# Output groups of a local attention inside the loop of a dense one: from one block of 15 full-row matmuls to five pieces of row halves

## The chip, the cores and the metric

The kernel runs on one core of a Trainium2 chip. The core has five engines that run side by side, each on its own queue of instructions: TensorE (PE, matmuls, with its weight loads as PEld), VectorE (DVE), ScalarE (ACT), GpSimd (POOL) and SyncE (SP), which here issues the DMA transfers. An engine works its queue off in order; it waits at an instruction until the semaphores say that its inputs are there and its output buffer is free. Matmuls write to PSUM, which has eight banks of 128 partitions x 512 columns of fp32; ACT and DVE read PSUM, POOL does not.

The metric is the device time of one execution in microseconds (us); lower is better. The time given is the median of several runs.

## What is computed

Two attention blocks over 2048 positions of 640 features, with 32 heads of 20, whose outputs stand side by side. Attention A looks at eight earlier positions, two apart; attention B at all positions.

```python
def _A_ref(x, wqkv, wo):                      # W, dil = 8, 2
    q, k, v = split_heads(x @ wqkv)           # 32 heads of 20
    idx = pos[:, None] - arange(8) * 2        # masked where negative
    attn = softmax(where(mask, einsum("bhsd,bhswd->bhsw", q, kg) * scale, -1e9))
    o = einsum("bhsw,bhswd->bhsd", attn, vg)
    return merge_heads(o) @ wo

def _B_ref(x, wqkv, wo):
    q, k, v = split_heads(x @ wqkv)
    p = softmax(einsum("bhqd,bhkd->bhqk", q, k) * scale)
    return merge_heads(einsum("bhqk,bhkd->bhqd", p, v)) @ wo

return concatenate([a, b], axis=-1)
```

## The kernel before

All matmuls of the projections are made exact enough by splitting each operand into a rounded high part and the rest, and summing three products (`PASSES`: high x high, high x low, low x high). A projection of 640 features is five contraction chunks (`KC`) of 128, so one output group of 128 rows x 320 columns is 15 matmuls into one PSUM bank: `rows15`.

**Stages.** First come A's projections of q, k and v (stored to DRAM), then B's q and k, then B's values (`v_group`). In the last of these the 15 matmuls are already made as row halves where `halves` is set: the contraction rows 0 to 63 and 64 to 127 are two matmuls on two halves of the array, into two banks; ACT copies both out of PSUM and POOL adds them. Then comes the long loop, then a tail that finishes B and writes its output.

**The loop.** It runs B's attention in units of four heads by 512 queries by 128 keys: 512 steps in all, of which the loop makes 488. Each step needs four half-row matmuls of scores (PE, 62 contraction rows, 512 columns) with an exponential each on ACT, and one set of value matmuls (`b_pv`, eight in the trace). Every second step ends a sum of values, which ACT copies out and POOL adds to the running sum (braw). The scores need the maximum of each query, and that is computed 24 steps ahead (`LEAD`) with score matmuls of its own (60 rows, 512 columns), which DVE reduces over the columns: four halves to a step as well, and three small DMAs bring the maxima back as extra rows of q.

**The order is written out by hand** in the string `ORDER`, from line 955 on, which is read token by token. A token names what PE does next and the PSUM banks that it uses:

- S: two halves of scores, each with its exponential. M: two halves of maxima in neighbouring banks, with one reduction of 1024 columns. N: the same in any two banks, with two reductions of 512. Y: one half of scores and one of maxima, with one exponential and one reduction of 512. Each is a pair of matmuls on the two row halves of the array, at the same time.
- V: the next step. `begin(i)` (which calls `tick`, so that work laid down with `after(n, ...)` becomes due) and then the value matmuls, into the bank that the token gives, if any.
- F: one output group of A, into the bank that it names. j: one of the five transposes of a tile of A.

**Attention A in the loop.** A's local attention is elementwise work on POOL (`a_attention`), in units that `begin` deals out: it emits the next unit as long as POOL's planned time (`gp.us`, a sum over the instructions emitted so far) is less than the step's time plus `AHEAD`. DVE makes its softmax's maximum and reciprocal, ACT its exponential. A finished tile of 128 rows is transposed by DVE (`j`), goes through DRAM, is split by POOL into `aot` (one buffer, `turn_parts`), and is then in `ready_a`. Each tile gives two output groups (two halves of 320 columns), 32 in all. `a_out` makes one: a bank, `rows15`, and `store_rows` with ACT's copy into a tile "ro" (tag "r", three buffers) and, one step later, the store to DRAM. A group named by F before its tile is ready is kept in `owed` and made at the next V.

When all groups of A are made (`left_a`), B's output weights are loaded into the same buffers as A's (`load_out(wo_b, ...)`); they are used after the loop.

The profile puts nearly all instructions on line 66, the helper `emit` that records them, so they are told apart by their tiles: `mx<-ps_st` are reductions for maxima, `e<-ps_st` exponentials, `bq,bk` and `bk,bq` score matmuls for maxima or exponentials, `e,vb` values, `ww,aot` A's output groups, `ww,xn` and `ww,xl` B's values, `ro` the copied outputs, `braw` and `more` the sums of values, `akv`, `al` and `am` attention A's operands, scores and maxima.

Of the kernel before, what the change touches and what calls it, by code (L numbers as in the profile page):

```python
# [10 lines left out]
F32 = mybir.dt.float32  # L11
# [7 lines left out]
H = 32  # L19
# [3 lines left out]
KC = 5  # L23
# [47 lines left out]
def attention_pair(ctx, tc, xa, wqk_a, wv_a, wo_a, xb, wqk_b, wv_b, wo_b, oa, ob):  # L71
# [720 lines left out]
    def b_token(kind, ns):  # L792

        m = None
        if kind == "S":
            what = [s_half(), s_half()]
        elif kind == "Y":
            o = s_half()
            if m_open[0] is None:
                m_open[0] = m_two()  # L800
                what = [o, (*m_open[0], 1 - o[3])]
            else:
                m, m_open[0] = m_open[0], None
                what = [o, (*m, 1 - o[3])]
        else:
            m = m_two()
            what = [(*m, 0), (*m, 1)]
        b_two(what, ns if len(ns) == 2 else (ns[0], ns[0] + 1), kind == "M")
        if m:
            m_done(m)  # L810
# [43 lines left out]
    def v_group(n, half, s, halves=False):  # L854
# [13 lines left out]
        if halves:  # L868
            more = sb.tile([128, 320], F32, tag="r", bufs=3, name="more")
# [42 lines left out]
    outs = iter(())  # L912
    fill = []

    def out_piece():

        nonlocal outs
        if next(outs, 0) is None:
            return True
        outs = a_out(WO)  # L920
        return next(outs, 0) is None
# [6 lines left out]
    def begin(i):  # L928
# [31 lines left out]
        "Y06S52M3Y17V6S05jM3Y21VY70S52M3S16N70V5S41M2Y67VY04S36M1S75N04V3S27Y61N05VY74S06jM1jN35jF7jY06M1S35S74V0M5Y31"  # L960
        "S72VY73S64M1Y50V3Y47M1S65VY07M5S41Y23V0Y17M5S42VY71M3S25S06N17V2Y03S14M5VY70M3S15S26N07V1Y25S04N36VY07S25N43"
        "Y61V0Y72N54S36VY71M5S23N40F7Y61M2S45Y07V6Y51M2S04VY70M4S13Y26V7Y03M4S21VS06M2S14N57V0Y16N23S45VS74M5M1N03F7Y62"
        "S01M4Y73V6Y02M4S71VY70M2S14Y56V7Y04M2S15VY06M4S13Y72Y60V1Y75M3S26VY07S62S53jN41N70jF6jjjY70M1S35Y46V7Y05M1S34V"
        "Y03M5S41S72N30V4Y57S36M1VY07M5S31Y42V7Y03S61Y54VM2S04Y16V5S07M2Y46VY70M2S14S65N70V1S26M3Y75VY06S72M3Y51V0Y72"
        "S63M4VY71M2S64Y05V7Y64M2S01VY06M4S13Y72Y60V1S75M3Y26VY07S25M3S61Y07V2M3Y56S71VN03S74M5S12S07N34V1Y02S35M6VY02"
        "M3Y57N61Y20F5Y74S63M1Y05V7Y64M1S03VS06M4S31N72V0S36M4Y71VM2S76Y45V1Y07S26N34VY07M2S65Y41V7Y06M2S54VY06M4jS13j"
        "S27jN60jF1jY72S03M4Y61V7Y02M4S63VY06M1S35S74N60V3Y72S16M4VY70M1S64Y35V0Y74S16M2VY71M4S63Y20V7Y61M4S32VY06M2S14"
        "S75N60V1Y72S36M4VY07M2S64S51N70V6Y52M3S71VS70M1S53N46V7S05M1Y34VS05Y63Y21N74V0S13M5Y72VS13M5S74Y02V1Y73M5S24V"
        "Y07M2S46S51N70V4Y35M6S21VY05M1S37N64N50F3Y74M1S56Y03V7Y64S52M0VY63M4S20S71Y36V2M4S07N16VS05Y74Y31V2Y04M5S71V"
        "Y70S34M5Y12V7S03N64Y51VjS06jM4M2S17F0jjjY71S26M4Y03V7Y62M4S01VY06M2S14Y75V0Y16M2S74VY71M5S42S30N17V4Y35S62M0V"  # L970
        "Y73M5S20Y14V7S03M5Y21VY03S24M5Y17V0Y24M5S13VY74M1S36S05N47V3Y02S41M5VY70M1S46S35N07V4Y36M1S05VY07Y63S52M0S74"
        "N63V5S70M1Y64VS70M1Y36S45V7M1S03Y46VY05S13Y24N67V0S13M4Y62VS71M4Y63N20F7Y61S02M4Y73V6Y02M4S71VY70M2S14S56N07V1"
        "Y25S04N36VY07S25M3S61N07V2S36M4Y01VY73M4S06Y12V7Y06M4S31VY06M2S14Y75V6Y04M2S17VY05S71jM2jS46jN50jF7jY06S51M2"
        "Y74V0Y15M2S76VS71M4S63N02V7S61M4Y03VS62M0S54N73V6S50Y12Y74VM2S01Y45V7Y60M2S15VY06M4S31S27N60V3Y24M5S71VY70M1"
        "S46S35N07V4Y36M1S05VY07M5S31S42N70V3Y41M5S72VY70M1S46S35N07V4Y36M1S05VY07M5S31S42V7M0Y63S45VM0S26S34N57V2Y30"
        "S16N54VY70M5Y13N42F0Y71M5Y43S02V7Y04M5S12VY04M1S35Y76V0Y53M1S74VY73M5S42S01N37V4Y05S36M1VY07M5S31S42N70V3S41j"
        "M5Y72VS04jY71M5M2F0jjY71S26M4Y03V7Y62M4S01VY06M2S14S75N60V1Y72S36M4jVS07M2S64Y51V0M6S23Y41VY73S26M4S10N37V2Y16"
        "M4S30VY73M0S64Y52V7Y63M0S45VY62M3S50Y17V2Y65M3S01VY07M5S14S32N70V1S36M4Y72VY03S74M5S21N03V7S62Y54M0VY62S35N40"
        "N71S62V3S04M5Y72VS04M5Y71N23F0Y71M5Y42S03V7S01M5S43VM0S26Y54V3Y70M1S46VY07S45M1S63N70V4Y51M6S32VM0S25M6S34Y20"
        "Y15V3Y42M6S01VY02S14M6Y53V2Y01M6S45VjS01jM4M6S32jF0jjY71M4S63Y02V7Y61M4S03VY06M1S35S74N60V3Y72M5S41VY70M1S46"  # L980
        "S35N07V4Y36M1S05VY07M5S31S42N70V3S41M5S72VM0S74Y56V2Y73M0S46VY73M4S06S12N37V0Y16M4S32VY71M2S64Y05V7Y64M2S01V"
        "Y06M4S13S27N60V1Y25M3S76VY07M5S24S31N70V2Y36S75Y14VM6Y05S43V1Y02S76M4VN07M2M4S61F0Y71S62M4Y03V7Y62M4S01VY06M2"
        "S14S75N60V1Y72S36M4VY07M2S64S51N70V6Y52M3S71VS70M1S53N46V7S05M1Y34VS05Y63M1Y74V0S35jM1Y76VS53S74jM1N06F5jjjY07"
        "S61M2Y45V0Y17S62M3VY71M5S24S03N17V2Y06S15M3VY07M5S14Y32V7S01M5Y43VY02S16M4S37N02V1Y36M4S07VY06M2S74S15N06V7S41"
        "M2S05VY64S03M1V5Y46S70M1VY74S63M1S05N47V6Y03M1S54VY70M4S31Y26V7Y03M4S21VS06M2M4Y17F0Y16S52M3Y70V1Y26M3S75VY07"
        "M5S24S31N70V2S36M4Y71VY03S74M5Y12V0Y73M5S14VY71M2S46S50N17V4Y35M1S06VY07M5S31S42N70V3Y41M5S72VS70M1S46N53V7S04"
        "M1Y65VjS04jS36M1Y75jF0jjY71M2S46Y05V7Y64M2S01VY06M4S13Y72V0Y13M4S76VY71M2S64Y50V1Y76M2S45VY07M4S63S21N07V6S52"
        "M3Y01VY75M3S02Y16V7Y05M3S21VY02M5S14Y73V2Y01M5S47VY01M3S75S62N10V7Y63S45M1VY06M3S52S71N60V5Y74S63M1VS07M3S62"
        "Y51V0S74Y36M1VY74M5S31S02N47V3Y06S45M1VY07M4Y61N23F0Y71S26M4Y03V7Y62M4S01VY06M2S14S75N60V1Y72S63M4VY07M2S64S51"
        "N70V6Y52S73N41VY70S52M3Y16V7S05jM3Y21VS06jM3Y52N17F0jY16S52M3Y70V1Y26M3S75VS07M5S24Y31jV0jM5S72Y14VY73S26M4Y10"  # L990
        "V3Y27M4S61VY07S61M4S23N70V6Y51S72M3VY70M1S53Y46V7Y05M1S34VY03M5S41S72N30V4Y57S36M1VY07M5S31S42N70V3Y41M5S72V"
        "Y70S14M5S32N07V1Y63M4S02VY07M2S64S51Y70V6M2S54Y01VN75S42M0S36Y74V5Y32M0S67VY64M2M0Y75F6Y74S03M1Y56V7Y04M1S35V"
        "Y06M3S52S71Y60V5Y74M2S01VM6S04Y32V1Y07M5S24VY07S23Y46N51V7S06M2Y54VS06jS51jM2N47F0jjjY71S26M4Y03V7Y62M4S01VY06"
        "M2S14S75N60V1Y72S36M4VY07M2S64S51N70V6Y52M3S71VS70M1S53Y46V7M1S05Y63VY02S14M5V3Y70S21M5VY70S14M5S23N07V1Y26M4"
        "S03VY07M2Y64S51V0Y75S63M1VY74M5S31S02N47V3Y06S45M1VY07M4S61S32N70V6Y51M3S72VS70M1S53Y46V7Y05M1S36VY03S45M1M6"
# [122 lines left out]
```

## Time and profile before

| | |
|---|---|
| runs, median of 3 (lowest to highest) | 1767.14 us (1765.48 to 1768.25) |
| profiled execution | 1766.22 us |
| its span, first to last instruction | 1764.4 us |
| instructions | 32352 |
| granted TensorE clock | 0.999 |

How to read it. The profile shows one execution. A row of the engines gives busy time, its share of the span and the number of instructions. The slices of the page divide the span in 40 equal parts; each digit is the busy share in tenths:

```profile
PE   9999999999999999999999999999999999999999
PEld 8988888898344444444444444444444444444569
DVE  3100232368999999999999999999999999999300
ACT  4222322233999999999999999999989999999981
POOL 0000058335899999999999999999999985355242
```

The projections take the first ten slices, the loop the next 27 or so, the tail the rest. Matmuls are pipelined and their ends are modelled, so a busy PE is not PE at its peak. In a view of groups a row gives the number of instructions, their busy time (overlaps counted once), the mean of one in ns, and the idle time of the engine just before them with what ended it. In a timeline a row gives start, length, engine, operation and how many instructions it merges, with the idle time before it in brackets; the start of the next row minus this row's start is what the work cost the engine's queue, since the ends of pipelined instructions overlap the next ones.

### The profile page before, as it was taken

Reading aid. Unit: us, or ns where it says so; the run is one execution under the profiler, and the core shown is the slowest. Engines: PE = TensorE matmul, PEld = TensorE weight load, DVE = VectorE, ACT = ScalarE, POOL = GpSimd, SP = SyncE. Lnnn points to the kernel's source line nnn. Section 1 sums busy time; section 2 is a strip of 40 time slices with the busy share of each in tenths; the row PEclk is TensorE's granted clock in tenths of the full one; section 3 lists DMA queues with packets and bytes.
Section 4 is the critical chain, followed back from the end, with each engine's and each line's share of the span. In section 5 each row is a group of like instructions: output and inputs, shape, how many; then the busy total and the mean of one; then the engine's idle time right before and its main releaser. Section 6 shows DMA issues by size and latency. Waiting matters only on the chain.

```text
span 1764.4 us, 32352 instructions
## 1 busy us (share of the span) xinstructions
PE 1751.5 (99%) x11571; PEld 996.1 (56%) x11571; DVE 1336.5 (76%) x1813; ACT 1330.0 (75%) x2617; POOL 1228.0 (70%) x1096
## 2 busy tenths in 40 slices
PE   9999999999999999999999999999999999999999
PEld 8988888898344444444444444444444444444569
DVE  3100232368999999999999999999999999999300
ACT  4222322233999999999999999999989999999981
POOL 0000058335899999999999999999999985355242
PEclk9999999999999999999999999999999999999999
DMA  6333596863644454364445345453644432122123
GB/s 231 114 98 110 174 312 245 270 183 116 179 135 136 118 150 124 123 168 124 129 138 153 124 120 160 116 155 102 177 133 128 129 114 72 38 71 58 33 71 115
DMA packets 191194, 240.27 MB, mean 136 GB/s; under 512 B 89020, under 2 KB 115260, under 8 KB 190040
## 3 DMA queue, kind: packets, MB, share of 16 engines
q1 hardware_dynamic: 190456, 237.54, 44.6%
q8 instruction: 91, 1.49, 0.4%
q10 hardware_dynamic: 576, 0.66, 0.1%
q14 instruction: 71, 0.58, 0.1%
HBM read 173.21 MB, written 64.91 MB: 135 GB/s over the span
## 4 chain that ended last, share of the span: by engine, by line
PE 88%; POOL 6%; DMA 2%; DVE 1%; ACT 1%; issue 1%; SPq 0%; POOLq 0%; ACTq 0%; DVEq 0%
PE ps_st L66 88%; POOL akv L66 3%; POOL braw L66 1%; DVE mx L66 1%; ACT e L66 1%; DMA bk<-kb_d 1%; POOL ww L66 1%; SPq L66 0%; DMA stg<-wo_a 0%; DMA vb_d<-ve 0%; POOL aot L66 0%; POOL al L66 0%; DMA s_d<-braw 0%; DMA akv<-ka_d 0%; DMA qb_d<-pr 0%
## 5 line engine op out<-in xcount | busy, mean ns | idle before, releaser
L66 DVE TENSOR_REDUCE mx<-ps_st 128x1 f32<-128x512 f32 (+1 forms) x1491 | 1215.1, 881 | 37.5 <-PE ps_st L66 32.8
L66 ACT ACTIVATE e<-ps_st 128x512 f32<-128x512 f32 x2048 | 1063.6, 619 | 31.2 <-PE ps_st L66 12.9
L66 PE MATMUL ps_st<-bq,bk 62*128 62x512 f32 x2048 | 552.7, 439 | 2.7 <-DVE mx L66 1.2
L66 PE MATMUL ps_st<-e,vb 128*32 128x512 f32 x4096 | 543.0, 604 | 0.6
L66 PE MATMUL ps_st<-bk,bq 60*128 60x512 f32 x2048 | 532.5, 438 | 3.0 <-DVE mx L66 2.0
L66 PEld LDWEIGHTS ps_st<-bq,bk 62*128 62x128 f32 x2048 | 277.4, 184 | 446.3 <-ACT e L66 285.5
L66 POOL TENSOR_TENSOR braw<-braw,more 128x512 f32<-128x512 f32 x224 | 288.0, 1286 | 93.1 <-ACT more L66 92.9
L66 POOL TENSOR_TENSOR akv<-akv,aq 128x1280 f32<-128x1280 f32 x64 | 189.0, 2953 | 233.7 <-DVE w L66 233.7
L66 PEld LDWEIGHTS ps_st<-bk,bq 60*128 60x128 f32 x2048 | 248.8, 184 | 85.6 <-DVE mx L66 47.9
L66 POOL TENSOR_TENSOR akv<-akv 128x640 f32<-128x640 f32 (+3 forms) x304 | 282.4, 929 | 14.3
L66 ACT COPY ro<-ps_st 128x320 f32<-128x320 f32 (+2 forms) x124 | 61.3, 496 | 223.0 <-PE ps_st L66 173.7
L66 PEld LDWEIGHTS ps_st<-e,vb 128*32 128x32 f32 x4096 | 82.1, 108 | 153.0 <-ACT e L66 74.1
L66 POOL TENSOR_TENSOR akv<-akv,al 128x1280 f32<-128x1280 f32 x64 | 152.0, 2375 | 0.2
L66 ACT COPY more<-ps_st 128x512 f32<-128x512 f32 (+1 forms) x248 | 144.5, 583 | 2.3 <-PE ps_st L66 1.5
L66 PE MATMUL ps_st<-wc,xn 128*128 128x512 f32 (+1 forms) x576 | 133.4, 376 | 0.0
L66 PE MATMUL ps_st<-ww,xn 64*128 64x320 f32 (+1 forms) x1056 | 125.8, 311 | 0.4 <-ACT ve L66 0.4
L66 PEld LDWEIGHTS ps_st<-ww,xn 64*128 64x128 f32 (+1 forms) x1056 | 116.8, 187 | 14.1 <-ACT e L66 8.0
L66 PEld LDWEIGHTS ps_st<-wc,xn 128*128 128x128 f32 x576 | 106.3, 188 | 17.6 <-ACT xn L66 0.3
L66 PE MATMUL ps_st<-xn,w 128*128 128x512 f32 x480 | 115.8, 390 | 0.0
L66 PEld LDWEIGHTS ps_st<-xn,w 128*128 128x128 f32 x480 | 90.1, 188 | 19.4
L66 ACT CAST pr<-ps_st 128x512 fp32r<-128x512 f32 x40 | 23.5, 587 | 101.4 <-PE ps_st L66 101.4
L66 DVE TENSOR_TENSOR pr<-ps_st,pr 128x512 fp32r<-128x512 f32 x40 | 27.7, 692 | 92.7 <-ACT pr L66 92.7
(65 smaller groups left out, 1010.3 us busy)
## 6 DMA issues: line engine op xcount, KB each, us to landing
akv<-ka_d SPq DMA_DIRECT2D x128, 320.0 KB
akv<-va_d SPq DMA_DIRECT2D x128, 320.0 KB
kb_d<-pr SPq DMA_DIRECT2D x20, 512.0 KB
qb_d<-pr SPq DMA_DIRECT2D x20, 512.0 KB
bk<-kb_d SPq DMA_DIRECT2D x16, 640.0 KB
bq<-qb_d SPq DMA_DIRECT2D x64, 160.0 KB
rb<-s_d SPq DMA_DIRECT2D x128, 64.0 KB
stg<-xb SPq DMA_DIRECT2D x12, 512.0 KB
```

The costliest lines, as they stand in the source:

```text
L66: return self.tc.keep_in_program_order(op(*a, **k))
```

## The change

An output group of A in the loop is no longer one block. The token F is gone; a token H with two banks stands for one of five pieces of a group. A piece is one contraction chunk: three passes, each as two matmuls of 64 contraction rows on the two row halves of the array, into the two banks. All five pieces of a group name the same two banks and stand between two V, with S, M, N and Y tokens among them. After the fifth piece ACT copies both banks into two tiles, POOL adds them one step later, and the store is issued four steps later (before: one step after the copy). The tag "r" has four buffers instead of three, everywhere that it is used.

The order string is another one from step 37 or so on: where groups and transposes stand and which tokens with which banks surround them. Its counts, before and after: S 661 and 641, Y 630 and 670, M 509 and 530, N 152 and 111, V 488 and 488, j 80 and 80, F 32 and none, H none and 160. `b_token` is cut in two without a change of what it does.

```diff
     def store_rows(p, dst):
-        r = sb.tile([128, 320], F32, tag="r", bufs=3, name="ro")
+        r = sb.tile([128, 320], F32, tag="r", bufs=4, name="ro")
...
-    def a_out(W):
-
-        while ready_a and ready_a[0][0] <= now[0]:
-            _, t, ot = ready_a[0]
-            for half in range(2):
-                if half:
-                    ready_a.clear()
-                p = bank()
-                rows15(p, lambda xi, k: ot[:, xi, k], W[half])
-                store_rows(p, oa[t * 128:(t + 1) * 128, half * 320:half * 320 + 320])
-                left_a[0] -= 1
-                yield
+    unit = []
+
+    def out_chunk(ns):
+
+        if not unit:
+            unit[:] = [0, *ready_a[0][1:], left_a[0] % 2]
+        k, t, ot, half = unit
+        for i, (wi, xi) in enumerate(PASSES):
+            for r, n in enumerate(ns):
+                rows = slice(r * HALF, r * HALF + HALF)
+                pe.matmul(psb[:, n, :320], ot[rows, xi, k], WO[half][wi][rows, k],
+                          start=(k == 0 and i == 0), stop=(k == KC - 1 and i == 2))
+        unit[0] += 1
+        if unit[0] < KC:
+            return
+        unit.clear()
+        left_a[0] -= 1
+        if half:
+            ready_a.clear()
+        o, more = [sb.tile([128, 320], F32, tag="r", bufs=4, name="ro") for _ in range(2)]
+        for to, n in zip((o, more), ns):
+            act.copy(to, psb[:, n, :320])
+        after(1, pool, o, o, more, ALU.add)
+        after(4, sp.dma_start, oa[t * 128:(t + 1) * 128, half * 320:half * 320 + 320], o)
...
-        "Y06S52M3Y17V6S05jM3Y21VY70S52M3S16N70V5S41M2Y67VY04S36M1S75N04V3S27Y61N05VY74S06jM1jN35jF7jY06M1S35S74V0M5Y31"
...
+        "Y06S52M3Y17V6Y05M3S21VY70M1S53S46jY07V5jY41S32M6jVjM0S43H76H76Y52H76Y01Y34H76Y52H76jM0S34V5M6S32Y01VM6S42Y03V1"
+        "S24M6Y50VY24S73M5Y01V2Y73M5S04VM0S73Y46H52H52Y70Y13H52Y46H52Y70H52M3Y16V7S05M1Y34VY06S51M2Y47V0Y16S52M3VY71M5"
...
     def out_owed():
 
-        while owed:
-            given.append(owed[0])
-            if not out_piece():
-                given.clear()
-                break
-            owed.pop(0)
+        while owed and (unit or ready_a and ready_a[0][0] <= now[0]):
+            out_chunk(owed.pop(0))
...
-        elif kind not in "FV":
+        elif kind == "H":
+            owed.append(ns)
+            out_owed()
+        elif kind != "V":
             b_token(kind, ns)
-        elif kind == "F":
-            owed += ns
-            out_owed()
```

More of the change, by code (lines that the diff above doesn't have):

```diff
@@ L790, in m_done, with take @@
             max_end(u * NKB + NKB - 1)
-    def b_token(kind, ns):
+    def take(kind):
         m = None
@@ L807, in b_token @@
             what = [(*m, 0), (*m, 1)]
+        return what, m
+    def b_token(kind, ns):
+        what, m = take(kind)
         b_two(what, ns if len(ns) == 2 else (ns[0], ns[0] + 1), kind == "M")
@@ L868, in v_group @@
         if halves:
-            more = sb.tile([128, 320], F32, tag="r", bufs=3, name="more")
+            more = sb.tile([128, 320], F32, tag="r", bufs=4, name="more")
             act.copy(more, ps2[1][:, :320])
@@ L909, in attention_pair @@
     assert next(steps, None) is None
-    outs = iter(())
     fill = []
[L915 to L921, printed above, removed]
     WO_b = []
@@ new lines, in attention_pair @@
+        "N56S71VY72Y13H45Y06H45S72N13H45S06H45Y72H45M0Y63V2M4S01Y76VS01M4Y73V6Y02M4S17VY03H71N24S65H71Y03H71Y26H71Y54"
+        "H71M2Y06V5Y74S03M1VS07M3N62S51V0S73M4Y16VS73M1Y45V0Y76M1S34VY73M5S42S10N37V4S56M1Y03VY75S06M1Y34V7Y06S51M2Vj"
+        "S06jM4S13Y72jV0jY16S54M2jVY71M5S42S30N17V4Y35S62M0VY73M5S20S14N37V2Y01M5S34VY70M3Y15S62V7Y60S14M2M5S01VS04M2"
+        "S15M6V0S14M2M6S15VY14M2S57Y06V4Y51M2S70VY75M0S62S34N57V6Y03M1S54VY70M4Y31S26Y07V3Y24M5S01VY70Y14S25H36H36Y71"
+        "H36N02S45H36Y71H36Y04N52V7S61M3Y05VY61S02M3Y57V6Y02S13M4VY70M1S35Y46V0Y75M1S34VY73M5S42Y10V3Y47M5S21VY70H42S15"
@@ new lines, in attention_pair @@
+        "N36H42S70H42Y31H42Y57H42M0Y36V7Y52S01M3VY06M1S53Y47V6S50jM1S34jVjY70S51M2V4jY07S56M2jVY70S15M2S64N07V1M2S65Y04"
+        "VM5S72S03Y41M5N72S10V3S41M5Y70VM1S74S56N03V7Y24M0S65VY62S35M0Y47V6Y53M0S24VY75M2S40S16N57V4Y03M1S56VY07M5S31"
+        "S42N70V3Y41M5S72VM0S72S46N53V7M0S24Y65VM2S04H16H16Y75H16Y04Y23H16H16M4S70M2V1S74M5VM2S07H45Y61H45H45Y07Y32H45"
+        "Y61H45Y07N32V6S75M0Y43VY75S04Y12N63V7S02M4Y61VY02S36M4Y17V0Y62M4S13VY71M2S64S05N17V6Y04M2S51VY70M4S13S26N07V1"
+        "Y25M3S06VS07M5S24Y31V0jY72M5S14VjM2S71Y46V5jY70M2S16VY70S61M2S45N07V6Y41M2S05VY70S15Y42Y36S07M1jV5jY64M1S03V"
@@ new lines, in attention_pair @@
+        "VM2S16H50Y47H50Y13Y62H50Y74H50Y13H50M6Y42V1S03M4Y76VM2S07Y45V6Y70M2S14VY70M4S13Y26V0Y71M4S32VY71M2S64H50H50Y17"
+        "H50Y64Y32H50Y17H50M3Y62V1S07M5Y43VY07M5S42Y31V0Y72M5S43VY74M1S36Y05V4S37jM1Y60VS75jM1S63Y04jV7jM1S65Y43VM1S06"
+        "Y54V3Y07M1jS65VY07M5S41S23N07V4S56M1Y03VM5S70M1S34V7Y06M3S52M0S65VY62M3S50S71N26V5Y70M3S21VY07M1S63S45N70V6Y14"
+        "M2S75VY70M4S13S26N07V1Y25M3S06VY07M5S24S31N70V2Y36M4S71VY07Y16M4S32S70V1M2S46Y75VM2S04H67H67Y51H67Y04Y32H67Y51"
+        "H67M3Y02V5S67M0Y43VY72M0Y64S35V7Y63M0S25VY62M3S50Y71V6Y05M3S72VY70H51Y24H51Y06Y73H51Y24H51Y06H51M2Y74V0S15M6"
@@ new lines, in attention_pair @@
+        "Y23VY14S72M5Y30V1Y27M5S43VY07M3S25Y61V7S02jM3Y56VY02S13M4S67Y02jV1jM4S63Y27VjM4S03M6jS21V0Y25S43M6VS15M3M6S20"
+        "V1S25M3M6S02VY05M3S27S61N05V2S37Y64M0VS73M4S60N12V7Y63S45M0VY62M3S50S71N26V5Y70M3S21VY07M1S63S45N70V6Y14M2S75V"
+        "Y70S15Y42Y36N07V1S26M4S03VM6S05Y42V3N07S61N52VM6S01H45H45Y03H45Y21Y67H45Y03H45H21M6H21S03M4H21H21M6S03H21N54V0"
+        "Y73S12M5VS71M3S25N06V7S41M2Y05VS64M0S23N75V6S04M1Y73VS05M1S74N36V0Y71S25M3VY71M5S24Y03V1Y27M5S40VjY72M3S05S61"
+        "Y72jV0jM3S56jY12VY73S64M1S50N37V6S51jM3Y02VY71S05M3S26N71V0S25M3Y76VY51Y72Y34M5S01S72V3Y40S15M6VM0S24S75N63V2"
@@ new lines, in attention_pair @@
+        "Y70S16M4VY70S16M4Y32V0Y17M4S63VY71M2S64Y50Y17V6Y52S34M0VY75M2S40S16N57V4Y03M1S56VY07M5S31Y42V7Y03S61M4VY06S13"
+        "H24N57H24S06H24Y35H24Y70H24M5S31N07V2S36M4Y01VY73S04M5Y12V7Y03M5S41VY04M2S15Y76V0Y15M2S74VS71M5S42N30V7M5S41"
+        "Y23VY04M5H12Y37H12S04H12N35S60H12Y74H12Y36N05V7S64M1Y03VS46M1S05Y73V4jY06M1S35VjM6S03Y21V5jY04M6S31VjY04M2S17"
+        "Y65V4Y70M2S16VY70M5S13S24N07V1Y26S05M3VM6S05M3S21V0Y72M5jS14VY71S24M5S30N71V2Y36M4S70VY73S06M4M1S73V0Y74M5S31"
+        "S27M3VS12M5S74N03V1S27M5Y04VS73M5S02N14V7S06Y53M1VY06M3S57S21Y06V5Y74M2S61VN07S64M2S15S06N74V1Y02S73M5VY07M2"
@@ new lines, in attention_pair @@
+        "M3Y21VY06S52M3Y17V0Y62M3S15VY71H26Y35Y04H26Y71H26Y35H26Y70H26M3Y15V7S60M1Y34VY06S51M2Y47V0Y16S52M3VY71M5S24Y03"
+        "V1Y27S64N50VN72S36H54Y01H54Y73H54Y62Y01H54H54M6Y32V0Y15M6S43VY15M3S27Y06V5Y12S74N30VY76S41M2Y05V6Y74M2S10VY75"
+        "M0S42H36H36Y75H36Y42H36Y70H36M4Y21V7Y06S52M3VY06M1S53Y74V0Y35M1S76VY73M4S62S10N37V6S51M3Y02VY71S05M3S26N71V0"
+        "S25M3Y76VY15M3S72S60N15V7S64M2Y01VY64S05M2S17N64V0S15M2Y76VY15S74M2Y60V1Y75M2S46VY07M4S63Y21V0Y73M4S62VS71M2"
+        "S64N05V7S63M1Y04VS35Y06M1S74N36V5S70M1Y43VY07S64M1S35N07V6S41M2Y05VY74M2S01S56N74V0Y15M2S76VY71M4S63S02N71V6"
@@ L1014, in attention_pair @@
+        "S05M3Y72VY05M3S71S26N05V7Y41M2S06VY01S64Y53S72N01V6M3S50Y71VM3S05M1S76")
     owed = []
     def out_owed():
-        while owed:
-            given.append(owed[0])
-            if not out_piece():
-                given.clear()
-                break
-            owed.pop(0)
+        while owed and (unit or ready_a and ready_a[0][0] <= now[0]):
+            out_chunk(owed.pop(0))
     i = 0
@@ L1078, in attention_pair @@
         out_matmuls(p, qc, n, (KC - 1,))
-        r = sb.tile([128, 320], F32, tag=("r", "p")[n > 1], bufs=(3, PB)[n > 1], name="ro")
+        r = sb.tile([128, 320], F32, tag=("r", "p")[n > 1], bufs=(4, PB)[n > 1], name="ro")
         (act.copy if n % 2 else dve.tensor_copy)(r, p[:, :320])
```

77 lines of the change are left out of this document (24 added, 53 removed).

## The prediction

> **What bounds the kernel now.** I read the page from the top (busy shares, slices, chain), then the stretches, then the groups of the busiest engines, then single moments. The page alone points to PE:
>
> ```profile
> PE 1751.5 (99%) x11571; PEld 996.1 (56%) x11571; DVE 1336.5 (76%) x1813; ACT 1330.0 (75%) x2617; POOL 1228.0 (70%) x1096
> PE 88%; POOL 6%; DMA 2%; DVE 1%; ACT 1%; issue 1%; SPq 0%; POOLq 0%; ACTq 0%; DVEq 0%
> ```
>
> PE is busy for 99% of the span and 88% of the chain. Both count pipelined matmuls whose ends are modelled, so the stretches must decide. The first row below is the loop before the first output group, the second the loop with the groups, the third the loop after them, the fourth the tail without maxima (columns: stretch, length, then each engine's busy time):
>
> ```profile
> 430.00:530.00 100.00, 98.79 (x659) 43.16 (x659) 96.20 (x128) 91.29 (x183) 92.05 (x85) 0.98 0.53 152
> 530.00:1560.00 1030.00, 1025.77 (x7054) 463.81 (x7054) 1010.45 (x1400) 956.92 (x1894) 937.49 (x816) 1.00 0.44 126
> 1560.00:1646.00 86.00, 85.59 (x588) 34.87 (x584) 85.02 (x115) 83.19 (x165) 48.56 (x49) 1.00 0.22 63
> 1646.00:1764.40 118.40, 114.27 (x799) 86.01 (x792) 8.26 (x16) 71.40 (x147) 35.89 (x34) 1.00 0.26 81
> ```
>
> The loop lasts some 1216 us (430 to 1646), 2.49 us for each of its 488 turns. In it DVE is busy 96.20 + 1010.45 + 85.02 = 1191.7 us and idle 24.3; ACT is idle 84.6 and POOL 137.9. Does PE have room? One turn's values, and a scores run, show what its work costs start to start:
>
> ```profile
> 902.30 1.07 PE L66 MATMUL ps_st<-e,vb 128*32 128x512 f32 x8
> 903.29 0.50 PE L66 MATMUL ps_st<-bq,bk 62*128 62x512 f32 x1
> ...
> 396.12 0.65 PE L66 MATMUL ps_st<-bk,bq 60*128 60x512 f32 x4
> 396.61 1.92 PE L66 MATMUL ps_st<-ww,xn 64*128 64x320 f32 x24
> 398.36 0.60 PE L66 MATMUL ps_st<-ww,xl 64*128 64x320 f32 x6
> 398.80 0.67 PE L66 MATMUL ps_st<-bk,bq 60*128 60x512 f32 x4
> ```
>
> Eight value matmuls take 903.29 - 902.30 = 0.99 us, a pair of half-row matmuls (396.61 - 396.12) / 2 = 0.245. A turn needs one such eight and on average four pairs: 0.99 + 0.98 = 1.97 us of 2.49, and 0.16 more for its share of the groups. PE has about 0.36 us a turn to spare. So in the loop DVE sets the time, with 2% of slack, and the other engines only matter where they let it run dry.
>
> A rule of the Trainium skill bears on this choice: Trace Analysis ("Perfetto Trace Analysis", section "Identifying the Most-Contended Engine") says that matmul occupancy is no good measure of nearness to the roofline, because PE's instructions are pipelined. By it PE's 99% is no bound and DVE is; without it PE is the bound and the second rival below is the forecast.
>
> **What the change removes: the long block.** In the loop an output group is 15 full-row matmuls in one piece. One of them, as PE, ACT and DVE saw it:
>
> ```profile
> 880.62 2.47 PE L66 MATMUL ps_st<-ww,aot 128*128 128x320 f32 x15
> 883.02 0.50 PE L66 MATMUL ps_st<-bq,bk 62*128 62x512 f32 x1
> ...
> 883.12 0.43 ACT L66 COPY ro<-ps_st 128x320 f32<-128x320 f32 x1 [1.59 <-PE ps_st L66]
> ...
> 880.27 2.92 DVE L66 TENSOR_REDUCE mx<-ps_st 128x1 f32<-128x512 f32 x3
> 883.11 0.48 DVE L66 STREAM_TRANSPOSE turn<-ao 128x128 f32<-128x128 f32 x2
> ```
>
> The block holds PE 883.02 - 880.62 = 2.40 us. ACT starves for 1.59 of it, but DVE lives through it on maxima laid up before. Where the stock was short, DVE paid:
>
> ```profile
> 1538.75 1.82 DVE L66 TENSOR_REDUCE mx<-ps_st 128x1 f32<-128x512 f32 x2 [1.87 <-PE ps_st L66]
> ...
> 1559.20 3.02 DVE L66 TENSOR_REDUCE mx<-ps_st 128x1 f32<-128x512 f32 x4 [1.22 <-PE ps_st L66]
> ...
> 1406.89 0.60 DVE L66 TENSOR_REDUCE am<-al 128x32 f32<-128x256 f32 x1 [2.22 <-POOL al L66]
> ```
>
> The first two follow the groups at 1535.8 and 1556.2. All of DVE's waits for PE in the stretch with the groups, from the view of the PSUM tile:
>
> ```profile
>   PE ps_st L66: 11.9, 31
> ```
>
> So 11.9 us in 31 waits is the most that a smoother supply can give back there; the third row is a wait for POOL, which nothing in the change removes.
>
> How much smoother is it? I counted both orders between tokens that feed DVE (M, N, Y), with 0.99 for a V, 0.245 for a pair, 2.40 for an old group, and for a new piece a fifth of the half-row run above, (398.80 - 396.61) / 5 = 0.44. Old: 62 silences over 1.6 us, 32 of them (the groups) of 2.65 to 2.89. New: 20 over 1.6, none over 1.73. The group's own PE time falls from 2.40 to 2.19, and the run above goes from half-row scores into half-row pieces and back without a gap, so cutting it in five costs PE nothing. Per turn with a group, old: 32 turns need 32 x (0.99 + 2.40) + 263 pairs x 0.245 = 172.9 us of PE and carry 289 halves of maxima, which last DVE 289 x 2.49 / 4 = 179.9. New: 30 turns (two hold two groups) need 30 x 0.99 + 32 x 2.19 + 259 x 0.245 = 163.2 and carry 287, 178.7. The margin doubles, 7.0 to 15.5. I take half of the 11.9 as given back: **-6.0**. Ends: nothing, and all of the loop's idle from 530 on, (1030 - 1010.45) + (86 - 85.02) = **-20.5**; below nothing stands in the rivals.
>
> **What the order adds or removes by itself.** Both orders hold 1952 halves of scores, 1952 of maxima, 488 V and 80 transposes. The maxima are packed otherwise: 530 reductions of 1024 columns for 509, 892 of 512 for 934.
>
> ```profile
> L66 DVE TENSOR_REDUCE mx<-ps_st 128x2 f32<-128x1024 f32 x509 | 616.5, 1215 | 3.0 <-PE ps_st L66 2.0
> L66 DVE TENSOR_REDUCE mx<-ps_st 128x1 f32<-128x512 f32 x933 | 602.4, 682 | 18.0 <-PE ps_st L66 14.2
> ```
>
> Busy time by count is 1.211 and 0.646: 21 x 1.211 - 42 x 0.646 = 25.4 - 27.1 = **-1.7**, all on DVE, so all on the path. By the means (1215 and 682, which overlap) it is -3.1.
>
> **What is hidden.** Each group gets a second ACT copy and a GpSimd addition:
>
> ```profile
> L66 ACT COPY ro<-ps_st 128x320 f32<-128x320 f32 x32 | 13.7, 427 | 47.6 <-PE ps_st L66 47.6
> ...
> L66 POOL TENSOR_TENSOR ve<-ve,more 128x320 f32<-128x320 f32 x24 | 19.3, 812 | 74.8 <-ACT more L66 73.0 <-DMA vb_d<-ve 1.7
> ...
> SPq L66 <- ACT ro L66: 183.1, 31, 14.4
> ```
>
> ACT: 32 x 0.427 = 13.7 us, on an engine with 84.6 idle in the loop, 47.6 of them before these very copies: nothing on the path. If that cover were gone, 13.7. POOL: 32 x 0.812 = 26.0 us. POOL is 91% busy from 530 to 1560, but a half empty after that (48.56 of 86), and attention A's work is dealt out by POOL's planned time: the additions push it back by 26 us, ten turns, and the last group moves from turn 450 to 458 of 488. Attention B's output weights, loaded after it, are needed only from turn 488. Nothing, while POOL keeps up; behind a late addition stand akv's products, A's softmax (for which DVE waits: the 2.22 above, once) and the braw sums. The upper end: such a wait at each of 15 softmaxes, 15 x 2.22 = 33.
>
> The store moves from one turn after the copy to four turns behind, after the addition. On SP's queue that is past the akv fetches, the q and k loads and the maxima's stores; the queue now stands 183.1 us in 31 waits for the copies because the store is issued early, so moving it back frees the queue rather than blocks it. Its number, 32, stays. Behind it wait akv loads (POOL) and the maxima's way back, needed 24 turns later. The r buffers go from three to four: two groups in one turn need just four. All of this I take at nothing.
>
> **Sum.** 1.7 + 6.0 = 7.7 less. The profiled execution took 1766.22 (span 1764.4 and 1.8 around it), 0.92 below the median of the runs, 1767.14. 1766.22 - 7.7 = 1758.5, and on the runs' median **1759.4**.
>
> **Rivals.**
>
> 1. *No change, 1764 to 1770.* DVE's small waits are spread over all of the loop (31 with a mean of 0.38), and a new order has as many of its own; or pieces come before their group is ready, are owed, and run together at the next V, so that the block stays a block. Then the packing alone is left, -1.7: 1765.4. For it: 20 silences of 1.73 remain, and during a group two of eight banks are gone. Chance 0.22.
>
> 2. *PE is the bound after all.* Then 32 x (2.40 - 2.19) = 6.7 counts, 1760.4; or, with all of the loop's idle won back, 1767.1 - 1.7 - 20.5 = 1744.9. For the first the chain's 88%, against it PE's spare 0.36 us a turn. Below 1750: 0.08.
>
> 3. *Slower: the banks.* A group holds two banks through some ten tokens, and the sums of the values one more; five are left for scores and maxima, where before a block held one bank for 2.40 us. If DVE cannot have a second maximum waiting while PE does an eight and a pair (0.99 + 0.245 + 0.245 = 1.48), it runs dry by what it lacks: a 512 reduction in hand lasts 0.646, so up to 0.83 a group, 32 x 0.83 = 27: 1767.1 - 1.7 + 27 = 1792 at worst. It decides from (1.7 + 3.5) / 32 = 0.16 a group on, and half of the worst, 0.4, gives 1778. Against it: the orders put M or N, two halves, right before most of the longer silences. Chance 0.10.
>
> 4. *Slower: evacuation.* Two banks must be emptied where it was one. If ACT had no room, its 13.7 us would count in full, with no gain beside the packing: 1767.1 - 1.7 + 13.7 = 1779. ACT's 84.6 us of idle time speak against it. A POOL that falls behind (up to 33) ends in the same region. Chance 0.06. On this the Trainium skill speaks against the change: TensorEngine Tiling (Array Packing), section "PSUM Bottleneck", warns that tiling speeds up TensorE but not the emptying of PSUM, so that the copies may become the bottleneck; by it the time would be this rival's, while by the row's idle time the sum stands.
>
> **How the numbers follow.** The forecast case (DVE stays the bound, 3.5 to 17 us gained) has 0.54. 0.2% is 3.5 us, about what a measurement of this kernel can tell from no change. Faster by more: 0.54 + 0.08 = 0.62; within: 0.22; slower: 0.10 + 0.06 = 0.16. The range leaves out 0.08 below 1750 and the slower cases' upper two thirds: 1750 to 1771.
>
> **What would show it.** Right: ACT's wait before the ro copies falls from 47.6 to under 15, DVE's idle time from 530 to 1646 from 20.5 to about 14, its reductions are 530 and 892, the tail after the last maximum still takes 118 us, matmuls of 64 rows from aot come in runs of six with pairs of scores between. Wrong: DVE waits for PE inside the new groups (rival 3), am waits for al more than once (rival 4), or DVE's idle time stays at 20 (rival 1).

## The result: 9 us less, and where they came from

The changed kernel takes **1758.29 us** (median of 5 runs, 1756.04 to 1760.11) against 1767.64 for the kernel before: ratio 0.9947, 95% interval 0.9932 to 0.9961. The profiled execution took 1756.04, 10.2 less than the profiled one before.

The loop up to the last reduction of maxima, and the tail behind it, before (columns: stretch, length, then busy time of PE, PEld, DVE, ACT and POOL):

```profile
430.00:1649.30 1219.30, 1212.76 (x8304) 543.01 (x8304) 1194.95 (x1645) 1134.70 (x2246) 1079.38 (x950) 1.00 0.43 123
1649.30:1764.40 115.10, 111.66 (x781) 84.83 (x781) 4.98 (x11) 68.10 (x141) 34.62 (x33) 1.00 0.27 84
```

The same two stretches after:

```profile
430.00:1639.10 1209.10, 1197.67 (x8783) 547.38 (x8783) 1192.85 (x1624) 1146.20 (x2278) 1104.99 (x982) 1.00 0.43 124
1639.10:1754.30 115.20, 111.68 (x782) 84.86 (x782) 4.98 (x11) 68.10 (x141) 34.65 (x33) 1.00 0.26 83
```

All of the gain lies in the loop; the tail is the same to 0.1 us. DVE's idle time in the loop fell from 24.35 to 16.25 us, 8.1 of the 10.2; the other 2.1 is busy time. From 530 to the last reduction the idle time fell from 20.5 to 13.7. What DVE waited for after, in the view of the PSUM tile over 530 to 1560 (before: 11.9, 31):

```profile
  PE ps_st L66: 5.4, 10
```

Over the whole loop, three waits before (time, number, longest), and the same three after:

```profile
DVE mx L66 <- PE ps_st L66: 16.2, 40, 2.1
DVE am L66 <- POOL al L66: 2.2, 1, 2.2
...
PE ps_st L66 <- DMA bq<-mdr: 0.7, 1, 0.7
```

```profile
DVE mx L66 <- PE ps_st L66: 8.0, 17, 1.4
DVE am L66 <- POOL al L66: 3.6, 1, 3.6
...
PE ps_st L66 <- DMA bq<-mdr: 3.6, 3, 1.8
```

So the waits for PE halved, and two others grew: DVE's one wait for POOL, and PE's for the DMA that brings maxima back.

Where the waits for PE stand in the timelines says more than their sum. Before, from 530 on, 24 of DVE's waits end 2.9 to 3.0 us behind the start of a group, 10.1 us together, and ten others are 2.4. After, four waits of 0.16 to 0.27 stand in a group, at its start or right behind it, 0.8 us together. The five longest after, 4.5 us together, stand behind three stops of PE, at 1215 and 1295 for the maxima's DMA and at 1429, which is followed below. So nearly all of what the block cost DVE is gone, and more than half of what is left is new.

A group after the change, on PE:

```profile
646.82 0.60 PE L66 MATMUL ps_st<-ww,aot 64*128 64x320 f32 x6
647.26 0.42 PE L66 MATMUL ps_st<-bk,bq 60*128 60x512 f32 x2
647.49 0.42 PE L66 MATMUL ps_st<-bq,bk 62*128 62x512 f32 x2
647.73 0.63 PE L66 MATMUL ps_st<-ww,aot 64*128 64x320 f32 x6
```

Six matmuls hold PE for 647.26 - 646.82 = 0.44 us, and pairs of scores follow without a gap. The groups of DVE and ACT that answer to those before:

```profile
L66 DVE TENSOR_REDUCE mx<-ps_st 128x2 f32<-128x1024 f32 x532 | 642.7, 1215 | 3.0 <-PE ps_st L66 1.7
L66 DVE TENSOR_REDUCE mx<-ps_st 128x1 f32<-128x512 f32 x892 | 576.0, 681 | 8.8 <-PE ps_st L66 6.3
...
L66 ACT COPY ro<-ps_st 128x320 f32<-128x320 f32 x64 | 24.6, 449 | 0.1
```

ACT no longer waits before the copies (47.6 us before, 0.1 now), but its waits for PE before the exponentials grew, so that about half of that time moved and did not go. Before and after:

```profile
ACT e L66 <- PE ps_st L66: 12.9, 52, 1.2
```

```profile
ACT e L66 <- PE ps_st L66: 38.6, 79, 3.2
```

### The profile page after: what moved, and what is told of

Same layout as the page of the kernel before. It is cut to its first block, busy times and chain, and to the rows that moved or that the text cites. A ratio compares the mean times of both kernels' runs of the same rounds, so it can differ in the third digit from the quotient of the medians.

```text
span 1754.3 us, 33331 instructions
## 1 busy us (share of the span) xinstructions
PE 1736.7 (99%) x12051; PEld 1000.7 (57%) x12051; DVE 1335.1 (76%) x1792; ACT 1341.2 (76%) x2649; POOL 1253.5 (71%) x1128
## 3 DMA queue, kind: packets, MB, share of 16 engines
q8 instruction: 94, 1.54, 0.4%
## 4 chain that ended last, share of the span: by engine, by line
PE 70%; POOL 11%; DVE 10%; DMA 5%; issue 2%; ACT 1%; SPq 1%; POOLq 0%; DVEq 0%; ACTq 0%
PE ps_st L66 70%; DVE mx L66 10%; POOL akv L66 6%; POOL braw L66 3%; ACT e L66 1%; SPq L66 1%; DMA bq<-qb_d 1%; DMA stg<-wo_a 1%; DMA bk<-kb_d 1%; DMA akv<-va_d 1%; POOL ao L66 1%; POOL aot L66 1%; POOL ww L66 0%; POOL al L66 0%; DMA vb_d<-ve 0%
## 5 line engine op out<-in xcount | busy, mean ns | idle before, releaser
L66 ACT ACTIVATE e<-ps_st 128x512 f32<-128x512 f32 x2048 | 1069.2, 618 | 56.9 <-PE ps_st L66 38.6
L66 PE MATMUL ps_st<-bq,bk 62*128 62x512 f32 x2048 | 563.3, 437 | 7.8 <-DMA bq<-mdr 3.6
L66 PE MATMUL ps_st<-bk,bq 60*128 60x512 f32 x2048 | 551.3, 437 | 4.1 <-DVE mx L66 2.4
L66 PEld LDWEIGHTS ps_st<-bq,bk 62*128 62x128 f32 x2048 | 282.3, 184 | 416.7 <-ACT e L66 267.6
L66 PEld LDWEIGHTS ps_st<-bk,bq 60*128 60x128 f32 x2048 | 257.8, 184 | 108.5 <-DVE mx L66 54.0
L66 ACT COPY ro<-ps_st 128x320 f32<-128x320 f32 (+2 forms) x156 | 72.2, 491 | 175.4 <-PE ps_st L66 125.8
L66 PEld LDWEIGHTS ps_st<-ww,xn 64*128 64x128 f32 (+1 forms) x1056 | 116.0, 186 | 13.7 <-ACT e L66 7.1
L66 PE MATMUL ps_st<-ww,aot 64*128 64x320 f32 x960 | 99.4, 308 | 0.0
```

The lines of the kernel that those rows point to most:

```text
L66: return self.tc.keep_in_program_order(op(*a, **k))
```

## The experiments

Each ratio is against the kernel before on the same chip; for the changed kernel it is 0.9947. A difference of 0.001 is 1.8 us.

### The pieces and the halves

**block_half**: the five pieces run together at the place of the first.

```diff
-            owed.append(ns)
-            out_owed()
+            pieces[0] += 1
+            if pieces[0] % KC == 1:
+                owed += [ns] * KC
+                out_owed()
```

> The changed kernel with all five pieces of a group made at the place of the first: same order, same two banks, same row halves, same two copies and addition, but PE is held for some 2.2 us as before. If the gain comes from cutting the block (DVE runs dry behind it), DVE's waits for PE in the loop rise from 8.0 us to 16 or more and the time goes back by 5 to 20 us, to 1763 to 1778: the new order lays up no stock of maxima ahead of a group, so it may be worse than before. If the gain comes from the order elsewhere or from the row halves, it stays at 1757 to 1760.

Measured: 1810.62, ratio 1.0234 (1.0217 to 1.0251), 52 us more than with the pieces apart. The block on PE, DVE behind it, and DVE's waits for PE in the loop (8.0 in 17 with the pieces apart):

```profile
642.78 2.38 PE L66 MATMUL ps_st<-ww,aot 64*128 64x320 f32 x30
...
645.47 1.89 DVE L66 TENSOR_REDUCE mx<-ps_st 128x1 f32<-128x512 f32 x3 [1.39 <-PE ps_st L66]
647.99 2.42 DVE L66 TENSOR_REDUCE mx<-ps_st 128x1 f32<-128x512 f32 x3 [0.63 <-PE ps_st L66]
```

```profile
DVE mx L66 <- PE ps_st L66: 55.2, 57, 1.9
```

In this order no stock of maxima stands ahead of a group, and DVE runs dry by 1.39 us behind one block; its waits for PE are 47 us more than with the pieces apart. The direction was expected, the size was not.

**pieces_full**: five pieces of three full-row matmuls, the rest of the load kept.

```diff
-            for r, n in enumerate(ns):
-                rows = slice(r * HALF, r * HALF + HALF)
-                pe.matmul(psb[:, n, :320], ot[rows, xi, k], WO[half][wi][rows, k], ...)
+            pe.matmul(psb[:, ns[0], :320], ot[:, xi, k], WO[half][wi][:, k], ...)
...
-        for to, n in zip((o, more), ns):
+        for to, n in zip((o, more), (ns[0], ns[0])):
...
-        after(1, pool, o, o, more, ALU.add)
+        after(1, pool, more, o, more, ALU.add)
```

> The changed kernel with its five pieces, but each of three matmuls over the full 128 contraction rows into one bank; both copies read that bank and GpSimd's addition is kept with a result that nobody reads, so ACT's and POOL's load is as in the changed kernel. If the row halves matter because pieces of another shape between half-row pairs cost PE a gap at each border (0.43 - 0.23 = 0.2 us going in and 0.24 - 0.15 = 0.09 coming out, before), each piece costs some 0.3 us more, 160 x 0.3 = 48 us of PE, of which PE's spare time hides a part: 1763 to 1790. If only the cutting matters, it stays at 1757 to 1760.

Measured: 1804.94, ratio 1.0210 (1.0193 to 1.0227), 47 more. Its pieces in PE's timeline, then DVE's waits for PE in the loop:

```profile
641.31 0.41 PE L66 MATMUL ps_st<-bq,bk 62*128 62x512 f32 x1
641.66 0.70 PE L66 MATMUL ps_st<-ww,aot 128*128 128x320 f32 x3
642.29 0.50 PE L66 MATMUL ps_st<-bq,bk 62*128 62x512 f32 x1
```

```profile
DVE mx L66 <- PE ps_st L66: 44.8, 109, 1.4
```

Three full-row matmuls hold PE for 0.63 us instead of 0.44, and the pair before them for 0.35 instead of 0.24: some 0.3 us a piece, 160 times, and nearly all of it arrives in the time. Above the range that was expected, because less was hidden.

**block_full**: the new order with the old group, one block, one copy, no addition.

```diff
-        for to, n in zip((o, more), ns):
-            act.copy(to, psb[:, n, :320])
-        after(1, pool, o, o, more, ALU.add)
-        after(4, sp.dma_start, ...)
+        store_rows(psb[:, ns[0]], oa[t * 128:(t + 1) * 128, half * 320:half * 320 + 320])
```

(with the edits of the two runs above)

> The new order with the old group at the place of its first piece: 15 full-row matmuls in one block into the first of the two banks, one copy, the store one step later, no addition. It undoes all but the order, the tokens' packing and the two reserved banks. If the cutting and the halves are the gain, 1763 to 1785, near the run with the block of halves and a little above it (2.40 against 2.19 us of PE a group), less what POOL's 26 us give back. If the order itself is the gain, 1757 to 1760.

Measured: 1810.72, ratio 1.0240 (1.0224 to 1.0255). The order alone is no gain: it costs 43 us without the pieces it was written for. In pieces the halves are worth 47 us. The two blocks come out alike (1810.62 with halves, 1810.72 full), but that is no test of the halves alone: the full block is longer on PE (2.40 against 2.19 us), and it is without the second copy and POOL's addition, which costs some 6 us (no_addition, below). What this can't tell either is what the best order for a block of halves, or for full-row pieces, would give.

### What sets the loop's time

**split_max**: every second reduction of 1024 columns made as two of 512.

```diff
-        b_two(what, ..., kind == "M")
+        turns[0] += kind == "M"
+        b_two(what, ..., kind == "M" and turns[0] % 2 == 0)
```

> The changed kernel with every second M token's reduction of 1024 columns made as two of 512: DVE gets 265 times 2 x 0.598 - 1.131 = 0.065 us (start to start in the loop), 17 us, by busy time and count 265 x (2 x 0.646 - 1.211) = 21 us; nothing changes for PE, ACT and POOL. If DVE sets the loop's time, the whole comes through: 1774 to 1780. If PE or POOL does, under 5 us: 1758 to 1763.

Measured: 1760.27, ratio 0.9958 (0.9943 to 0.9973): 2 us, not 17; by the intervals anything up to some 6 is possible. Its DVE groups, then its loop as one stretch (DVE's waits for PE in it are 4.3 us in 11):

```profile
L66 DVE TENSOR_REDUCE mx<-ps_st 128x1 f32<-128x512 f32 x1422 | 880.8, 679 | 4.6 <-PE ps_st L66 3.4
L66 DVE TENSOR_REDUCE mx<-ps_st 128x2 f32<-128x1024 f32 x267 | 323.7, 1213 | 1.4 <-PE ps_st L66 0.9
```

```profile
430.00:1642.00 1212.00, 1201.84 (x8783) 539.87 (x8783) 1201.85 (x1889) 1147.33 (x2278) 1105.31 (x982) 1.00 0.44 124
```

DVE's busy time rose by 9.0, its idle time fell by 6.1 (16.25 to 10.15), and the loop grew by 2.9. The likely reason, argued and not shown, is that of two short reductions the first hands PE a bank back some 0.5 us sooner than one long one (0.68 against 1.21 us), so that the next scores are there sooner.

**dve_adds**: DVE reads the second bank and adds, instead of ACT's second copy and POOL's addition.

```diff
-        for to, n in zip((o, more), ns):
-            act.copy(to, psb[:, n, :320])
-        after(1, pool, o, o, more, ALU.add)
...
+        act.copy(o, psb[:, ns[0], :320])
...
+        after(2, sp.dma_start, ...)                 # the store, two steps earlier
+        late.append((ns[1], o))
...
+        if late:                                    # in b_token, after b_two
+            n, o = late.pop(0)
+            dve.tensor_tensor(o, psb[:, n, :320], o, ALU.add)
```

> The changed kernel without ACT's second copy and GpSimd's addition: DVE adds the second bank to the copied first one, after the token that follows the last piece; POOL's planned time is advanced as if it added. POOL is 26 us lighter, ACT 10 us, DVE 32 additions of some 0.49 us heavier, 16 us. If DVE's time counts in full, 1758 - 6 + 16 = 1768. If DVE takes extra work as it did the split reductions (17 us for 2), 1752 to 1758.

Measured: 1769.39, ratio 1.0008 (0.9999 to 1.0016).

```profile
L66 DVE TENSOR_TENSOR ro<-ps_st,ro 128x320 f32<-128x320 f32 x32 | 15.4, 480 | 0.0
```

Against the kernel without the addition (below, 0.9910) that is 0.0098, 17 us, for 15.4 us of DVE work. The two loops differ by 17.2 us as well (430 to 1651.0, and to 1633.8), of which 13.1 is busy time of DVE and 4.1 idle time. The idle part has its own cause: DVE's additions hold their bank, and PE waits for it:

```profile
PE ps_st L66 <- DVE ro L66: 7.8, 16, 0.9
```

So DVE's time counts nearly in full where the work only takes time. That the split reductions were cheap because they are not only that is the likely reading, and not shown.

**four_passes**: a fourth product in each piece.

```diff
-        for i, (wi, xi) in enumerate(PASSES):
+        for i, (wi, xi) in enumerate((*PASSES, (1, 1))):
...
```

> The changed kernel with a fourth pass (low times low) in each piece: 160 more pairs of row halves, 0.146 us each, 23.4 us of PE in the turns with groups and nothing else. If DVE is the bound with room on PE, the groups' margin of 15.5 us takes most: 1758 to 1768. If what PE needs in a group's turn comes through in full, as the full-row pieces suggest (0.63 against 0.44 us and a gap, some 48 us, and 47 were lost), 1776 to 1782.

Measured: 1776.74, ratio 1.0049 (1.0032 to 1.0067): 18 of the 23.4 us arrive. DVE's waits for PE become many and short:

```profile
DVE mx L66 <- PE ps_st L66: 14.9, 50, 0.7
```

In the turns with groups PE is as much the bound as DVE. Of the 19.6 us that the profiled loop is longer, 12.5 are idle time of DVE and 7.1 busy time (1199.95 against 1192.85) of the same reductions; they probably stand further apart, since busy time counts overlaps once.

### What POOL's addition costs

**no_addition**: the two halves are not added.

```diff
-        after(1, pool, o, o, more, ALU.add)
+        after(1, busy, 0.2 + 320 * 0.00212)      # gp.us += us
```

> The changed kernel without GpSimd's addition of the two halves (the first half alone is stored, so attention A's output lacks contraction rows 64 to 127 of each chunk); POOL's planned time is advanced as if it were there, so the work is dealt out alike. If the 26 us of additions are why POOL lags behind its plan (7 to 10 us behind the copies where before had 5 to 6), DVE's 3.6 us wait for the softmax operand and PE's waits for the maxima's way back (1.8 and 0.9 us) go: 1748 to 1754. If they come from elsewhere, 1757 to 1760.

Measured: 1752.40, ratio 0.9910 (0.9892 to 0.9928), 0.0037 or 6 us below the changed kernel, as expected (by the intervals, 2 to 11). DVE's waits in its loop; PE's are 4.2 us for DVE and 1.8 for ACT, and none is left for the maxima's DMA:

```profile
DVE mx L66 <- PE ps_st L66: 2.9, 11, 0.6
DVE am L66 <- POOL al L66: 1.7, 1, 1.7
```

DVE's idle time in the loop is 9.6 us, 6.6 less than in the changed kernel, and the timelines say where: 1.9 in the softmax wait itself, 2.0 in the waits behind the stop of PE that it brings on, and 2.2 behind the two stops for the maxima's DMA.

What such a wait does can be followed in the changed kernel from 1429 on. DVE's queue stands at the softmax maximum of A's last tile; PE gets no bank and stops; and then its clock is lower (timelines of DVE and PE, then stretches, whose third number from the right is the granted clock):

```profile
1430.89 0.59 DVE L66 TENSOR_REDUCE am<-al 128x32 f32<-128x256 f32 x1 [3.60 <-POOL al L66]
...
1432.13 0.79 PE L66 MATMUL ps_st<-bq,bk 62*128 62x512 f32 x1 [3.14 <-DVE mx L66]
1434.84 1.93 PE L66 MATMUL ps_st<-e,vb 128*32 128x512 f32 x8
...
1437.57 1.82 DVE L66 TENSOR_REDUCE mx<-ps_st 128x1 f32<-128x512 f32 x2 [1.44 <-PE ps_st L66]
```

```profile
1432.00:1439.40 7.40, 7.27 (x32) 2.88 (x32) 5.96 (x8) 4.27 (x8) 7.32 (x6) 0.55 0.64 209
1439.40:1445.00 5.60, 5.60 (x48) 2.95 (x46) 4.96 (x8) 5.14 (x12) 4.20 (x5) 1.00 0.00 0
```

For 7.4 us the clock is 0.55 on average (0.50 from 1432 to 1438), the eight value matmuls take 1.93 us instead of 1.07, and DVE waits again. The Trainium skill has a rule that bears on this: TensorE: Matmul & The Clock Gate, section "What's actually happening", says that an idle window of some 3.4 us puts the array at half clock until a busy window has passed. The rows agree with it in the half clock and in its release. They differ in the pause: here it is a little shorter, 3.14 us, in ahead_0 (below) one of 2.96 was enough, and in one_matmul (below) the clock fell without any.

**cast_on_act**: the rounding of A's transposed tile moved from POOL to ACT.

```diff
-        gp.tensor_copy(ot[:, 0], r)
+        act.copy(ot[:, 0], r)
+        gp.us += 0.2 + 640 * 0.00081
...
-        ready_a.append((now[0] + 5, t, ot))
+        ready_a.append((now[0] + 3, t, ot))
...
-            turned.append((now[0] + 3, t, r))
+            turned.append((now[0] + 5, t, r))
```

> The changed kernel with the rounding of attention A's transposed tile (640 columns, 16 times, 0.72 us each on POOL) made by ACT instead, two turns later than before, POOL's planned time advanced as if it still did it: 11.5 us less on POOL, some 11 us more on ACT, groups at the same places. If POOL's lag costs what leaving out the additions gave back (26 us off POOL, 5.9 us off the time), 11.5/26 of it: 2 to 4 us less than the changed kernel, 1754 to 1757. If ACT stalls on the tile's DMA, or the lag does not matter, 1757 to 1764.

Measured: 1759.82, ratio 0.9956 (0.9943 to 0.9969), no change. DVE's waits are as before this edit:

```profile
DVE mx L66 <- PE ps_st L66: 8.0, 24, 1.5
DVE am L66 <- POOL al L66: 3.0, 1, 3.0
...
PE ps_st L66 <- DMA bq<-mdr: 0.2, 1, 0.2
```

11.5 us off POOL did not buy their share of the 6. They did take away PE's stops for the maxima's DMA (3.6 us before this edit), but not the softmax wait; and DVE waits for PE as long as before, in more and smaller waits elsewhere. That those come from the 11 us that ACT now does more is likely, and not shown.

**cast_and_adds**: the edits of cast_on_act and dve_adds together.

> Both reliefs of POOL at once, 37 us less on POOL: the cast on ACT and the additions on DVE. If POOL's lag is what the changed kernel still pays for and DVE takes the additions cheaply, 1748 to 1755, the fastest of all. If DVE's additions count in full, 1764 to 1768.

Measured: 1773.45, ratio 1.0033 (1.0020 to 1.0046), above both ranges. DVE's additions count, and the cast on ACT costs some 4 us beside them (1.0033 against 1.0008) where it was to give some.

**ahead_0**: A's work dealt out later.

```diff
-AHEAD = 2.4
+AHEAD = 0.0
```

> The changed kernel with AHEAD = 0 instead of 2.4: attention A's work is dealt to POOL's queue 2.4 us later, one turn; every group is still ready at its token. If POOL's lag costs DVE and PE the waits of 3.6, 1.8 and 0.9 us and what follows them, 1750 to 1755. If not, 1757 to 1760; if POOL now runs dry, attention A ends later without a cost as long as the weights come in time.

Measured: 1766.00, ratio 0.9980 (0.9970 to 0.9990), slower, against the expectation. The edit also changes what stands before what on POOL's queue, and so the way back of the maxima. Early in the loop PE stops for it:

```profile
514.04 0.74 PE L66 MATMUL ps_st<-bq,bk 62*128 62x512 f32 x2 [2.96 <-DMA bq<-mdr]
```

The granted clock was 0.81 from 511 to 518 (0.50 from 516 to 518), and DVE waited 2.53 and 1.54 us. As a test of POOL's lag the run is inconclusive, since it did not relieve POOL.

### What the groups still cost

**one_matmul**: each group cut to its first pair.

```diff
-        for i, (wi, xi) in enumerate(PASSES):
+        for i, (wi, xi) in enumerate(PASSES[:k == 0]):
...
```

> The changed kernel with each group's 30 matmuls cut to the first pair (attention A's output is then one product of fifteen); copies, addition and store stay. It says what the groups still cost. If they are hidden but for DVE's waits in them (under 3 us), 1753 to 1758. If PE's time in the group turns still comes through, up to 32 x 2.05 = 66 us less: 1692 to 1740.

Measured: 1766.87, ratio 0.9993 (0.9982 to 1.0004): 8 us more with 28 of 30 matmuls gone, which neither case expected. One group's turn in PE's timeline:

```profile
935.09 0.38 PE L66 MATMUL ps_st<-ww,aot 64*128 64x320 f32 x2
935.25 0.50 PE L66 MATMUL ps_st<-bq,bk 62*128 62x512 f32 x1
935.53 0.49 PE L66 MATMUL ps_st<-bk,bq 60*128 60x512 f32 x1
936.03 0.50 PE L66 MATMUL ps_st<-bq,bk 62*128 62x512 f32 x1
...
939.58 1.94 PE L66 MATMUL ps_st<-e,vb 128*32 128x512 f32 x8
```

Three stretches of it, of 1 us each (columns as above; the third number from the right is the granted clock):

```profile
937.00:938.00 1.00, 1.00 (x7) 0.55 (x5) 1.00 (x2) 1.00 (x3) 1.00 (x2) 1.00 0.67 259
939.00:940.00 1.00, 1.00 (x7) 0.35 (x10) 1.00 (x2) 0.88 (x3) 1.00 (x2) 0.50 0.03 8
941.00:942.00 1.00, 1.00 (x6) 0.50 (x4) 0.13 (x1) 0.00 (x0) 1.00 (x3) 0.50 0.05 16
```

With the pieces gone PE has only scores to make, at the pace of the banks that come free, with starts up to half a microsecond apart. A few microseconds of that and the granted clock falls to 0.50; the values take 1.94 us, and DVE is out of work (0.13 us busy in the last row).

**one_pass**: one product of three in each piece.

```diff
-        for i, (wi, xi) in enumerate(PASSES):
+        for i, (wi, xi) in enumerate(PASSES[:1]):
...
```

> The changed kernel with one pass in place of three in each piece (high times high; attention A's output is coarser): a group has 5 pairs of row halves, spread as before, 0.15 us each. Full groups take 1758, groups of a single pair 1767, with a granted clock of 0.64 to 0.85 around the groups. If the falling clock is the reason for that, a third of the pieces' work that still comes at every piece keeps the clock up at more groups than the single pair: DVE's waits under 15 us and 1748 to 1760. If the emptied turn itself is badly fed, whatever the clock, it is 1760 to 1767 like the single pair.

Measured: 1757.35, ratio 0.9932 (0.9915 to 0.9949), no different from the full pieces, with 10.5 us of DVE's waits for PE and a mean clock of 0.997 (one_matmul: 20.7 and 0.987). It came out as the falling clock has it. From 530 on, DVE's longer waits stand behind the same three stops of PE as in the changed kernel. So two thirds of the pieces' work are free, one pass more than the three costs 18, and taking nearly all of it away costs 8.

## Why the prediction was right, point by point

- **The block and its waits (-6.0 of 11.9).** Right: the waits of that row fell by 6.5, to 5.4, and those of the whole loop by 8.2. The cut, not the order elsewhere, is what does it: the waits behind the groups went from 10.1 to 0.8 us, and with the block back in this order the time is 52 us above the changed kernel and 43 above the kernel before. The size was partly luck: half of 11.9 was a choice without a sum behind it, the waits behind the groups gave back more, 9.3, and the new stops of PE took 4.5 again. That the halves cost PE nothing at the borders held (0.44); full-row pieces would have cost 47 us more, and the change would have been a loss of 37.
- **The packing (-1.7, "all on DVE, so all on the path").** This term was mis-sized. The counts were right (892 reductions of 512; 532 of 1024 in the loop, two of them outside the order, as before), but 265 such swaps cost 2 us, so 21 are worth some 0.2. The step that failed is the price: 0.08 us a swap from busy time by count, put on the path in full. In split_max a swap took 0.034 us of busy time (9.0 / 265), and most of that was made up by less idle time. DVE's busy time did fall by 2.1, but it is no measure of the packing alone: four_passes, with the same reductions, has 7.1 more.
- **"Nothing, while POOL keeps up".** It did not quite. The additions took 0.87 us each and 27.8 in all (26.0 in the prediction), and cost some 6 us, by no_addition. The prediction had the mechanism (the softmax for which DVE waits) and an upper end of 33, but put it at nothing. So the cut brought some 15, and a good third of that went back: of DVE's idle time that no_addition saves, 3.9 us hang on one softmax wait and 2.2 on the maxima's way back. Whether those maxima were late on POOL or on SP's queue, which waits for the addition too, stays open.
- **DVE as the bound, PE with 0.36 us to spare.** Right on average, too simple in the groups' turns. There the margin of 15.5 us was wrong: it priced DVE's work at the loop's pace of 2.49 us a turn, which contains the idle time itself and DVE's other work. Of 23.4 us more on PE only some 5 were hidden. With less on PE than now, though, DVE is the bound there too: one_pass takes 320 pairs away, some 47 us of PE by four_passes' price, and is no faster.
- **ACT, the tail, the stores.** Right: the copies' waits fell to 0.1 (though those before the exponentials grew, to 38.6), the tail is 115.2 against 115.1 (the prediction's 118 counted from 1646), the groups are runs of six.
- **The rivals.** Rival 1 had the waits stay as many as they were, and they fell. Rival 2, PE as the bound, has 1760.4 as its first time, which the number alone cannot tell from the forecast; one_pass speaks against it. How much of the gain comes from a group's shorter time on PE (2.19 against 2.40 us) was not separated from the cutting. The scores' banks (rival 3) did not bite: the largest wait for PE in the loop is 1.44, and that one stands behind the stop at 1429, not in a group, where the waits are 0.8 us in all. Evacuation (rival 4) was not ACT but, as its last clause had it, POOL, and at 6 us, where that clause went up to 33.

In sum: 7.7 forecast, 9.4 measured (10.2 between the two profiles), from a larger gain than expected and a cost that was put at nothing. That they nearly cancel is luck; that the gain came from DVE's waits behind the block is not.

## What to carry to other kernels

In this kernel a block of matmuls of another shape cost twice: it silenced the engine that empties PSUM, and it paid at its borders. Cut into pieces of the same tiling as their neighbours it cost neither, but the cut, the tiling and the order around it are worth something only together, so try them together. And count what the new form hands to a third engine: POOL was busy 89% of the loop before (1079.38 of 1219.30) and off the path, and 26 us more on it still cost 6.

## What was not expected of the hardware

The granted clock fell to 0.50 without a stop of PE: in one_matmul some 4 us of sparse pairs were enough (rows above). After a true stop of 3.14 us it was 0.50 for some 6 us more. Work that fills PE's gaps can thus be cheaper than none: one pass in each piece is some 10 us faster than a single pair in each group.
